# A layer of dilated window attention plus a bilinear GLU on one core: the first 20 microseconds reordered

## The chip, the core and the metric

The kernel runs on one core of a Trainium2 chip. The core has a matrix engine (TensorE, PE in the profile; its weight loads are shown apart as PEld), a vector engine (VectorE, DVE), an engine for activations and copies (ScalarE, ACT), a general one (GpSimd, POOL) and one that only issues transfers (SyncE, SP). ScalarE and GpSimd issue transfers too. All transfers run on 16 DMA engines; those issued from SP go through one queue. An engine works through its instructions in order and waits on semaphores for the others.

The metric is the time of one execution in microseconds of the device; lower is better. The kernel before took 264.84 us, the median of 3 runs (264.83 to 265.99).

## What is computed

Two branches read the same normalized input and are added to it. S = 2048 tokens, D = 640, F = 1536, 32 heads of 20; each token attends to itself and to 7 tokens before it, two apart.

```python
def reference(A_x, A_wqkv, A_wo, B_x, B_w_gate, B_w_up, B_w_down):
    def _A_ref(x, wqkv, wo):
        B, S, D = x.shape
        H = 32; Dh = D // H
        W, dil = 8, 2
        qkv = (lambda x, *d: x.transpose(*d))((x @ wqkv).reshape(B, S, 3, H, Dh), 2, 0, 3, 1, 4)
        q, k, v = qkv[0], qkv[1], qkv[2]
        ...
        logits = jnp.einsum("bhsd,bhswd->bhsw", q, kg) * scale
        logits = jnp.where(mask[None, None, :, :], logits, -1e9)
        attn = _softmax(logits, axis=-1)
        o = jnp.einsum("bhsw,bhswd->bhsd", attn, vg)
        return (lambda x, *d: x.transpose(*d))(o, 0, 2, 1, 3).reshape(B, S, D) @ wo

    def _B_ref(x, w_gate, w_up, w_down):
        g = jnp.einsum("bsd,df->bsf", x, w_gate)
        u = jnp.einsum("bsd,df->bsf", x, w_up)
        h = g * u
        return jnp.einsum("bsf,fd->bsd", h, w_down)

    x = A_x
    xn = _layernorm(x, axis=-1)
    return x + _A_ref(xn, A_wqkv, A_wo) + _B_ref(xn, B_w_gate, B_w_up, B_w_down)
```

Inputs, weights and the result are bfloat16. The inputs fit the core's memory piece by piece; nothing is shared with other cores.

## The kernel before

The tokens are cut into 16 tiles of 128 (x0 to x15) and 4 chunks of 512. Each step of the work is an object with an engine, a cost and the steps that it depends on. A planner (`Plan.order`) computes a due time for every step, backwards from the end, then simulates the engines and always takes, for the engine that is free first, the ready step that is due first. The costs and some earliest ends (`floor`) are written by hand. The order that it finds is the order of the program; no loop is left at run time. "after" puts one step behind another in the plan without a wait between them on the chip.

- A tile of x is loaded (L166), its mean and variance come from two `bn_stats` of 320 columns each (L251) and one `bn_aggr` (L257), epsilon is added (L259), GpSimd raises the sum to the power -0.5 (L265), and VectorE subtracts and multiplies (L270).
- The normalized tile is transposed into `xnT`: for the first chunk on TensorE, in two parts of 3 and 2 blocks (L345), which ScalarE copies out of PSUM (L351); for the other chunks by a DMA transpose that SP issues (L339).
- v comes from `xnT` and `wv` in two halves of 320 columns, five matmuls each (L438); ScalarE copies it (L444), and GpSimd stores it to `vD` in DRAM (L459). q and k come out transposed: five blocks each, five matmuls of 512 columns a block (L405), copied by ScalarE (L412).
- Attention of a chunk: eight products of q with shifted k on VectorE (L476), summed over the head's columns by TensorE with a matrix of ones (L490, two groups), copied (L503), transposed by DMA (L511), softmax on VectorE and ScalarE (L522 to L544); the values of eight positions are gathered from `vD` (L554, 1280 KB a tile), multiplied and summed on VectorE (L579 to L594), and transposed by DMA (L601).
- The GLU of a chunk: 12 blocks of gate and up matmuls of 512 columns (L621), copied (L626) and multiplied (L637). The last step of a tile adds the down projection (L662) and the attention's output projection (L665) in one PSUM bank, and VectorE adds x (L672).

Ahead of all this TensorE runs ten matmuls on zeros (L242) while the first tiles are loaded. The early transfers are spread over two queues. SP issues x0, x1, x2, then wq, x4 to x6, wk, x7, the DMA transposes of chunk 1, wg, x9 to x12, wu, the transposes of the first logits, then the gathered values. ScalarE issues the two column halves of wv, x3 and, later, x8, and loads the table for Exp. `hold` writes two elements of a weight tile so that its load waits for that write. PSUM has six banks under the name `ps`, which all matmuls but the logits' use in turn, and two under the name `pl` for the logits.

The lines that say where a wait or a place comes from:

```python
    HQ = inline("DVE", 0.08, hold(wq))
    WQ = load(10.1, wload(wq, A_wqkv[:, 0:D]), [HQ])
    ...
    qk(0, 0, CS)
    vproj(3)
```

Of the kernel before, what the change touches and what calls it, by code (L numbers as in the profile page):

```python
# [31 lines left out]
class Plan:  # L32
# [15 lines left out]
    def order(self):  # L48
# [4 lines left out]
        for s in reversed(self.steps):  # L53
            s.late = min([t.late for t in s.succ], default=0.0) - s.cost
        for s in self.steps:
            if s.urgent:
                s.late = -1e6 + s.idx
# [40 lines left out]
def kernel(  # L98
# [31 lines left out]
    NS = D // 2  # L130
    BF, F32 = dt.bfloat16, dt.float32
# [16 lines left out]
    mhalf = const.tile([P, 1], F32, name="mhalf")  # L148
    Ek = const.tile([P, KT, H], BF, name="Ek")
# [18 lines left out]

    X = {}
# [4 lines left out]
    def table():  # L174
        dm = sb.tile([P, 1], F32, name="dm", tag="dm")
        nc.vector.memset(dm[:], 0.0)
        nc.scalar.activation(dm[:], dm[:], ACT.Exp)
# [9 lines left out]
    def part(n):  # L187
        src = A_wqkv[:, 2 * D + n * NS : 2 * D + (n + 1) * NS].rearrange("(i p) f -> p i f", p=P)
        return lambda: nc.scalar.dma_start(out=wv[:, :, n * NS : (n + 1) * NS], in_=src)

    def hold(dst):
        return lambda: nc.vector.memset(dst[0:1, 0, 0:2], 0.0)

    X[0] = load(3.0, load_x(0))
    X[1] = load(3.8, load_x(1))
    X[2] = load(4.9, load_x(2))

    def consts0():
        wz = new("wz", [P, CS], BF, "gs", 5)
        nc.vector.memset(wz[:], 0.0)  # L200
        hold(wv)()
        nc.vector.memset(mhalf[:], -0.5)
        make_identity(nc, ident[:])
# [29 lines left out]
    WV = [add("ACT", 4.6, part(0), [C0], occ=0.45)]  # L233
    WV.append(add("ACT", 5.6, part(1), occ=0.45, after=[WV[0]]))
    X[3] = add("ACT", 5.0, load_x(3, nc.scalar), occ=0.45, after=[WV[1]])
    TB = add("ACT", 1.6, table, after=[X[3]])
    CZ = add("POOL", 3.0, consts_z, [C0], occ=1.2)

    def warm():
        ps = psum.tile([P, 512], F32, name="ps", tag="ps", bufs=6)  # L240
        for _ in range(10):
            nc.tensor.matmul(ps[:], lhsT=T["wz"][:, 0:P], rhs=T["wz"][:], start=True, stop=True)  # L242

    main = add("PE", 4.4, warm, [C0])


# [7 lines left out]
    def ln_aggr(t):  # L254
        def fn():
            mv = new(("mv", t), [P, nc.vector.BN_AGGR_DIM], F32, "mv", 6)
            nc.vector.bn_aggr(mv[:], T["st", t][:])  # L257
            ve = new(("ve", t), [P, 1], F32, "ve", 6)
            nc.vector.tensor_scalar(ve[:], mv[:, 1:2], scalar1=EPS, scalar2=None, op0=ALU.add)  # L259
        return fn  # L260
# [17 lines left out]
    def behind(s, a):  # L278
        s.after.append(a)
        s.deps.append(a)  # L280
        plan.steps.remove(s)
        plan.steps.append(s)
# [7 lines left out]

    def aggr_in(t, d):
        GL[t] = inline("DVE", 0.39, ln_aggr(t), [d], 0.35)
        RS[t] = add("POOL", 0.56, ln_rstd(t), [GL[t]])
# [4 lines left out]
    def ln(t):  # L298
        turn = [XT.get(t - (1 if t == CH else 2)), GL.get(t - 1)] if t < 2 * CH else []
        a = add("DVE", 0.48, ln_stats(t, 0), [X[t], GL.get(t - 3), *turn], occ=0.395)  # L300
        a = add("DVE", 0.48, ln_stats(t, 1), [a], occ=0.395)
        a = GL[t] = add("DVE", 0.39, ln_aggr(t), [a], occ=0.3)
        b = RS[t] = add("POOL", 0.56, ln_rstd(t), [a])
        XT[t] = add("DVE", 0.443, ln_apply(t), [b], occ=0.35)
# [13 lines left out]
    XDMA = 4  # L318
    GP = {}

    def transposes(t):
# [19 lines left out]
        def half(g0, g1, n):  # L341
            def pe():
                ps = new(("pst", t, n), [P, KT, P], BF, "ps", 6, psum)
                for g in range(g0, g1):
                    nc.tensor.transpose(ps[:, g, :], T["x", t][:, g * P : (g + 1) * P], ident[:])  # L345

            def ev():
                if n == 0:
                    slot()
                o, i = T["xnT", c][:, g0:g1, q * P : (q + 1) * P], T["pst", t, n][:, g0:g1, :]  # L350
                nc.scalar.copy(o, i)  # L351
            return pe, ev

        if t < CH:
            pa, ea = half(0, 3, 0)
            pb, eb = half(3, KT, 1)
            a = pe_main(0.17, pa, [XT.get((t, 0), XT[t])])
            TX[t] = add("ACT", 0.5, ea, [a], occ=0.42)
            ring.append(TX[t])
            a = pe_main(0.11, pb, [XT[t]])  # L360
            TT[t] = add("ACT", 0.42, eb, [a, TX[t]], occ=0.33)
            if t:
                behind(VE[t - 1][0], TT[t])
            ring.append(TT[t])
        elif t < XDMA:
            a = pe_main(0.28, pe, [XT[t]])
            TT[t] = add("ACT", 0.695, ev, [a], occ=0.6)
            ring.append(TT[t])
        else:
            if c == 1:  # L370
                a = TT[t] = chain[0] = add("SP", 3.0, dma, [XT[t]], occ=1.28, after=[chain[0]])
            else:
                a = TT[t] = add("SP", 2.8, dma, [XT[t], GP.get(c - 2)], occ=1.28, kb=200)
        if t + 5 < W:
            X[t + 5] = load((11.0, 11.5, 14.2)[t], load_x(t + 5), [a])
        elif t == 3:
            X[t + 5] = add("ACT", 6.0, load_x(t + 5, nc.scalar), [a], occ=0.45)
# [18 lines left out]
    def qk(c, lo, n, rs=(0, 1)):  # L396
        for r in rs:
            for j in range(KT):
# [20 lines left out]
                else:  # L419
                    pe_main(3 * one, lambda pe=pe: pe(0, 3), mine)  # L420
                    a = pe_main(2 * one, lambda pe=pe: pe(3, KT), [TT[t] for t in ts], banks=0)
# [6 lines left out]
    VE = {}  # L428

    def vproj(t, ns=(0, 1)):  # L430
        c, q = divmod(t, CH)
        evs = VE.setdefault(t, [])
        for n in ns:
# [15 lines left out]
            if t < 3 and n == 0:  # L449
                pe_main(3 * 0.136, lambda pe=pe: pe(0, 3), [TX[t], WV[n]])  # L450
                a = pe_main(2 * 0.136, lambda pe=pe: pe(3, KT), [TT[t]], banks=0)
            else:
                a = pe_main(KT * 0.136, lambda pe=pe: pe(0, KT), [TT[t], TX.get(t), WV[n]])
            e = add("ACT", 0.425, ev, [a, VS.get(t - 3), CZ], occ=0.35)
            ring.append(e)
# [12 lines left out]
    def prodlog(c):  # L468
# [13 lines left out]
        LASTPW[c] = PW[m]  # L482
        for g in range(2):
# [32 lines left out]
    def softmax(c, hf):  # L516
# [16 lines left out]
        e = add("ACT", 0.635, ex, [DD[n]], occ=0.54)  # L533
# [14 lines left out]
    def load_v8(t):  # L548
# [13 lines left out]
        if t < 3:  # L562
            SPLAST[0] = V8[t]
            V8[t].floor = (43.5, 0, 0)[t]
# [141 lines left out]
    a = st_in(0, 0)  # L706
    a = st_in(0, 1, a)
    aggr_in(0, a)
    a = st_in(1, 0)
    a = st_in(1, 1, a)  # L710
    HQ = inline("DVE", 0.08, hold(wq))
    WQ = load(10.1, wload(wq, A_wqkv[:, 0:D]), [HQ])
    X[4] = load(10.6, load_x(4))
    XT[0, 0] = inline("DVE", 0.31, ln_apply(0, 0, 3 * P), [RS[0]], 0.25)
    XT[0, 1] = inline("DVE", 0.26, ln_apply(0, 3 * P, D), [RS[0]], 0.2)
    XT[0] = XT[0, 1]
# [3 lines left out]
    vproj(0, (0,))  # L720
    a = st_in(2, 0)
    a = st_in(2, 1, a)
    apply_in(1)
    transposes(1)
    WK = load(13.6, wload(wk, A_wqkv[:, D : 2 * D]))
    aggr_in(2, a)
    vproj(0, (1,))
    vproj(1, (0,))
    a = st_in(3, 0)
    a = st_in(3, 1, a)  # L730
    apply_in(2)
    transposes(2)
    aggr_in(3, a)
    behind(VS[0], RS[3])
    vproj(1, (1,))
    vproj(2, (0,))
    apply_in(3)
    transposes(3)
    vproj(2, (1,))
    CE = add("POOL", 1.2, consts_e, [C0, RS[3]])  # L740
    CM = add("POOL", 1.1, consts_m, [CE])
    for t in range(CH, 2 * CH):
# [3 lines left out]
    for t in range(9, 13):  # L746
        X[t] = load(30.0, load_x(t), [TT[t - 5]])
    WL["u"] = load(36.0, wload(wu, B_w_up))
    qk(0, 0, CS)
# [9 lines left out]
    def attention(c):  # L759
# [3 lines left out]
        if c == 0:  # L763
            load_v8(0)
# [54 lines left out]
```

## Time and profile before

| | |
|---|---|
| median of 3 runs | 264.84 us (264.83 to 265.99) |
| profiled execution | 264.88 us |
| its span, first to last instruction | 263.2 us |
| first warm-up to the start of the q matmuls (L405) | 1.27 to 11.73 us |
| end of the last matmul, end of the span | 260.4, 263.2 us |
| x0, x1, x2 land | 3.15, 3.9, 5.7 us |
| halves of wv, wq, wk land | 5.2 and 7.0, 10.3, 13.9 us |
| DVE's products of chunk 0 (L476) | 23.3 to 34.7 us |

The span is what the profiler shows; some 1.7 us lie around it. Busy time is the time in which an engine executes; on TensorE matmuls overlap, so that a matmul's own duration is longer than the distance to the next one. What counts for its pace is that distance. A landing is the time when the semaphore of a transfer has all its counts. The chain of waits goes back from the last instruction and shows at each step what released it.

### The profile page before, as it was taken

What the parts mean: (1) busy time and instruction counts of PE and PEld (TensorE: products, weight loads), DVE (VectorE), ACT (ScalarE), POOL (GpSimd) and SP (SyncE); (2) the same over time, 40 slices, a digit from 0 to 9 for tenths busy, and PEclk for the clock granted to TensorE, in tenths of its full rate; (3) what the DMA queues carried; (4) which work ended last, traced back from release to release, by engine and by line L of the source; (5) the groups of instructions that cost most, each with busy time, mean ns of one, the idle gap of its engine ahead of it and who ended that gap; (6) DMA issues with size and microseconds to landing.
All of it is one profiled execution on the core that took longest, in us unless ns stands there. A gap on an engine that the chain in (4) does not pass through costs nothing.

```text
span 263.2 us, 4101 instructions
## 1 busy us (share of the span) xinstructions
PE 258.5 (98%) x1574; PEld 140.9 (54%) x1574; DVE 214.7 (82%) x337; ACT 106.0 (40%) x197; POOL 39.3 (15%) x84
## 2 busy tenths in 40 slices
PE   7999999999999999999999999999999999999995
PEld 2645455444677446444477554644456764445763
DVE  5775997799899999999999189999992999993221
ACT  2755557555200347455510155655541105554000
POOL 4651036000021121400001000420000004000000
PEclk9999999999999999999999999999999999999999
DMA  7998927999989149931167299451903985111001
GB/s 220 334 198 270 399 106 190 381 362 253 287 188 278 50 99 369 310 112 29 25 124 251 66 305 322 99 149 25 199 28 70 364 296 134 28 25 25 27 25 50
DMA packets 50707, 46.55 MB, mean 177 GB/s; under 512 B 24786, under 2 KB 47840, under 8 KB 50688
## 3 DMA queue, kind: packets, MB, share of 16 engines
q1 hardware_dynamic: 46704, 37.10, 50.1%
q0 software_dynamic: 2384, 8.05, 8.9%
q10 hardware_dynamic: 1600, 1.15, 1.4%
q8 instruction: 12, 0.20, 0.3%
q14 instruction: 7, 0.06, 0.1%
HBM read 35.39 MB, written 5.26 MB: 154 GB/s over the span
## 4 chain that ended last, share of the span: by engine, by line
PE 78%; DVE 11%; DMA 7%; SPq 1%; issue 0%; ACT 0%; DVEq 0%
PE ps L621 30%; PE ps L662 15%; PE ps L405 15%; DMA pv<-vD 7%; PE ps L438 7%; PE ps L665 6%; DVE pv L476 4%; DVE pv L579 3%; PE pl L490 3%; PE ps L242 2%; DVE xr L672 1%; DVE pv L588 1%; SPq L230 1%; DVE pv L592 1%; PE ps L345 0%
## 5 line engine op out<-in xcount | busy, mean ns | idle before, releaser
L621 PE MATMUL ps<-xnT,wg 128*128 128x512 bf16 x240 | 59.6, 379 | 0.0
L621 PE MATMUL ps<-xnT,wu 128*128 128x512 bf16 x240 | 59.6, 379 | 0.0
L662 PE MATMUL ps<-wd,hT 128*128 128x320 bf16 (+2 forms) x384 | 57.4, 299 | 0.0
L476 DVE TENSOR_TENSOR pv<-q,k 128x2560 bf16<-128x2560 bf16 x32 | 46.5, 1484 | 3.0 <-ACT k L412 3.0
L579 DVE TENSOR_TENSOR pv<-pv,a 128x5120 bf16<-128x5120 bf16 x16 | 45.1, 2820 | 3.0 <-DMA pv<-vD 2.9
L662 PEld LDWEIGHTS <-hT 128*128 128x128 bf16 x384 | 37.0, 98 | 16.5 <-issue 0.8
L626 ACT CAST gs<-ps 128x512 bf16<-128x512 f32 x48 | 28.2, 587 | 32.2 <-PE ps L621 32.2
L621 PEld LDWEIGHTS <-wu 128*128 128x128 bf16 x240 | 23.5, 98 | 28.3
L621 PEld LDWEIGHTS <-wg 128*128 128x128 bf16 x240 | 23.5, 98 | 27.7
L626 ACT CAST us<-ps 128x512 bf16<-128x512 f32 x48 | 28.2, 587 | 22.4 <-PE ps L621 22.0
L672 DVE TENSOR_TENSOR xr<-ps,xr 128x320 bf16<-128x320 f32 (+2 forms) x32 | 15.0, 486 | 24.5 <-PE ps L665 16.1
L665 PE MATMUL ps<-wo,oT 128*128 128x320 bf16 (+2 forms) x160 | 27.0, 299 | 0.0
L696 POOL DMA_DIRECT2D out_dram<-xr x14 | 7.6, 542 | 125.8 <-DVE xr L672 119.2
L588 DVE TENSOR_TENSOR pv<-pv 128x2560 bf16<-128x2560 bf16 x16 | 23.8, 1485 | 0.1
L438 PE MATMUL ps<-wv,xnT 128*128 128x320 bf16 x160 | 23.3, 300 | 0.4 <-ACT xnT L351 0.4
L412 ACT CAST q<-ps 128x512 bf16<-128x512 f32 x20 | 11.7, 585 | 27.8 <-PE ps L405 27.8
L637 DVE TENSOR_TENSOR hT<-gs,us 128x512 bf16<-128x512 bf16 x48 | 19.5, 419 | 4.0 <-ACT us L626 4.0
L405 PE MATMUL ps<-xnT,wq 128*128 128x512 bf16 x100 | 22.4, 379 | 0.0
L405 PE MATMUL ps<-xnT,wk 128*128 128x512 bf16 x100 | 22.2, 379 | 0.0
L438 PEld LDWEIGHTS <-xnT 128*128 128x128 bf16 x160 | 15.3, 98 | 7.5 <-ACT xnT L351 0.6
L665 PEld LDWEIGHTS <-oT 128*128 128x128 bf16 x160 | 15.5, 98 | 6.3
L444 ACT CAST v_t<-ps 128x320 bf16<-128x320 f32 x32 | 13.3, 429 | 7.4 <-PE ps L438 4.1
(54 smaller groups left out, 178.7 us busy)
## 6 DMA issues: line engine op xcount, KB each, us to landing
pv<-vD SPq DMA_DIRECT2D x16, 1280.0 KB, 10.0
vD<-v_t POOLq DMA_DIRECT2D x16, 160.0 KB, 4.5
xr<-in_A_x_dram POOLq DMA_DIRECT2D x16, 160.0 KB, 3.7
out_dram<-xr POOLq DMA_DIRECT2D x14, 160.0 KB, 3.5
wg<-in_B_w_gate_dram SPq DMA_DIRECT2D x1, 1920.0 KB, 8.1
wu<-in_B_w_up_dram SPq DMA_DIRECT2D x1, 1920.0 KB, 12.2
wd<-in_B_w_down_dram SPq DMA_DIRECT2D x1, 1920.0 KB, 17.7
x<-in_A_x_dram SPq DMA_DIRECT2D x11, 160.0 KB, 4.9
```

The source lines that it names most:

```text
L405: nc.tensor.matmul(T[key][:, 0:n], lhsT=(wk if r else wq)[:, i, j * P : (j + 1) * P], rhs=T["xnT", c][:, i, lo : lo + n], start=(i == 0), ...
L438: nc.tensor.matmul(T["psv", t, n][:, 0:NS], lhsT=T["xnT", c][:, i, q * P : (q + 1) * P], rhs=wv[:, i, n * NS : (n + 1) * NS], start=(i == ...
L444: nc.scalar.copy(T["v_t", t][:].rearrange("p (j h) -> p j h", j=Dh, h=H)[:, :, n * H // 2 : (n + 1) * H // 2], T["psv", t, n][:, 0:NS].rea ...
L476: nc.vector.tensor_tensor(T["pw", c, i // 2][:, i % 2, :, :], T["q", c][:], T["k", c][:, :, DIL * i : DIL * i + CS], ALU.mult)
L579: nc.vector.tensor_tensor(v[:].rearrange("p w (j h) -> p w j h", j=Dh, h=H), v[:].rearrange("p w (j h) -> p w j h", j=Dh, h=H), T["a", n][ ...
L588: nc.vector.tensor_tensor(v[:, 0:4, :], v[:, 0:4, :], v[:, 4:8, :], ALU.add)
L621: nc.tensor.matmul(ps[:], lhsT=(wu if r else wg)[:, i, f * P : (f + 1) * P], rhs=T["xnT", c][:, i, :], start=(i == 0), stop=(i == KT - 1))
L626: nc.scalar.copy(s[:], T[key][:])
L637: nc.vector.tensor_tensor(h[:], T["gs", c, f][:], T["us", c, f][:], ALU.mult)
L662: nc.tensor.matmul(ps, lhsT=T["hT", c, f][:, q * P : (q + 1) * P], rhs=wd[:, f, sl], start=(f == 0), stop=(f == FT - 1 and not wo_part))
L665: nc.tensor.matmul(ps, lhsT=T["oT", t][:, g, :], rhs=wo[:, g, sl], start=False, stop=(g == KT - 1 and f1 == FT))
L672: nc.vector.tensor_tensor(T["xr", t][:, sl], T["psD", t, n][:, 0:w], T["xr", t][:, sl], ALU.add)
```

## The change

1. x0 is loaded as two column halves of 320, each with its own transfer; each `bn_stats` waits for its half.
2. The halves of wv become row blocks 0 to 2 and 3 to 4, and they, x3 and x8 are issued by SP instead of ScalarE. SP's order is now x0 (two), x1, x2, wv (two), wq, x3 to x6, wk, x7, the transposes, wg, x8 to x12, wu. `hold` is gone. The value matmuls of x0 to x2 go through the row blocks in parts: blocks 0 and 1 of both column halves, block 2 of both, then blocks 3 and 4.
3. For x0 to x2, epsilon, power and add are replaced by a Sqrt with a bias on ScalarE and a reciprocal on VectorE. ScalarE loads the table for Sqrt first and the one for Exp after the first q columns.
4. The parts of the transposes on TensorE are 2 and 3 blocks, in the `pl` banks. x3 is transposed by DMA like later tiles.
5. q and k of chunk 0 are computed for 384 columns (x0 to x2) and then for 128 (x3).
6. The gathered values of tile 0 are issued right behind wu, ahead of the transposes of the logits.
7. Eight warm-ups, and a ninth behind the transposes of x0.
8. The planner walks the steps in the order of their dependences instead of the order of their making.

```diff
-        for s in reversed(self.steps):
+        todo = {s: len(s.succ) for s in self.steps}
+        work = [s for s in self.steps if not s.succ]
+        while work:
+            s = work.pop()
             s.late = min([t.late for t in s.succ], default=0.0) - s.cost
+            for d in s.deps:
+                todo[d] -= 1
+                if not todo[d]:
+                    work.append(d)
...
+    TA, VA = 2, 3
...
+    def load_x0(g):
+        def fn():
+            if g == 0:
+                new(("x", 0), [P, D], BF, "x", 5)
+            nc.sync.dma_start(out=T["x", 0][:, g * NS : (g + 1) * NS], in_=x_flat[0:P, g * NS : (g + 1) * NS])
+        return fn
...
     def part(n):
-        src = A_wqkv[:, 2 * D + n * NS : 2 * D + (n + 1) * NS].rearrange("(i p) f -> p i f", p=P)
-        return lambda: nc.scalar.dma_start(out=wv[:, :, n * NS : (n + 1) * NS], in_=src)
-
-    def hold(dst):
-        return lambda: nc.vector.memset(dst[0:1, 0, 0:2], 0.0)
-
-    X[0] = load(3.0, load_x(0))
+        i0, i1 = ((0, VA), (VA, KT))[n]
+        src = A_wqkv[i0 * P : i1 * P, 2 * D : 3 * D].rearrange("(i p) f -> p i f", p=P)
+        return lambda: nc.sync.dma_start(out=wv[:, i0:i1, :], in_=src)
+
+    X0 = load(2.75, load_x0(0))
+    X[0] = load(3.2, load_x0(1))
     X[1] = load(3.8, load_x(1))
-    X[2] = load(4.9, load_x(2))
+    X[2] = load(4.4, load_x(2))
+    WV = [load(5.5, part(0)), load(6.6, part(1))]
+    WQ = load(9.7, wload(wq, A_wqkv[:, 0:D]))
+    X[3] = load(10.1, load_x(3))
+    X[4] = load(10.5, load_x(4))
...
-        for _ in range(10):
-            nc.tensor.matmul(ps[:], lhsT=T["wz"][:, 0:P], rhs=T["wz"][:], start=True, stop=True)
+        new("wps", [P, 512], F32, "ps", 6, psum)
+        warming(8)
...
+    def ln_std(t):
+        def fn():
+            nc.scalar.activation(new(("std", t), [P, 1], F32, "ve", 6)[:], T["mv", t][:, 1:2], ACT.Sqrt, bias=epst[:])
+        return fn
+
+    def ln_inv(t):
+        return lambda: nc.vector.reciprocal(new(("rstd", t), [P, 1], F32, "rstd", 6)[:], T["std", t][:])
...
-    XDMA = 4
+    TPE = CH - 1
...
-        if t < CH:
-            pa, ea = half(0, 3, 0)
-            pb, eb = half(3, KT, 1)
...
+        if t < TPE:
+            pa, ea = half(0, TA, 0)
+            pb, eb = half(TA, KT, 1)
...
+        if c == 0:
+            load_v8(0)
         for g in range(2):
...
-    a = st_in(0, 0)
-    a = st_in(0, 1, a)
+    a = st_in(0, 0, X0)
+    a = st_in(0, 1)
     aggr_in(0, a)
+    inv_in(0)
+    XT[0, 0] = inline("DVE", 0.26, ln_apply(0, 0, TA * P), [RS[0]], 0.2)
+    XT[0] = XT[0, 1] = inline("DVE", 0.31, ln_apply(0, TA * P, D), [RS[0]], 0.25)
     a = st_in(1, 0)
     a = st_in(1, 1, a)
-    HQ = inline("DVE", 0.08, hold(wq))
-    WQ = load(10.1, wload(wq, A_wqkv[:, 0:D]), [HQ])
-    X[4] = load(10.6, load_x(4))
...
     transposes(0)
-    vproj(0, (0,))
+    pe_main(0.22, lambda: warming(1), banks=0)
+    vproj(0, (-1, 0))
...
-    for t in range(9, 13):
+    for t in range(8, 13):
         X[t] = load(30.0, load_x(t), [TT[t - 5]])
     WL["u"] = load(36.0, wload(wu, B_w_up))
-    qk(0, 0, CS)
+    qk(0, 0, TPE * P)
+    qk(0, TPE * P, P)
+    TE = add("ACT", 1.6, table(ACT.Exp), [Q[0][1]], occ=1.5)
     vproj(3)
```

## The prediction

> **What bounds the kernel now.** I read the page's busy times first:
>
> ```profile
> PE 258.5 (98%) x1574; PEld 140.9 (54%) x1574; DVE 214.7 (82%) x337; ACT 106.0 (40%) x197; POOL 39.3 (15%) x84
> ```
>
> TensorE (PE) is busy 258.5 of 263.2 us. The chain of waits, in order of time, shows from when on it never stops (start us, length us, what):
>
> ```profile
> 1.27 4.45 PE ps L242 x10
> 5.72 0.44 PE ps L345 x3
> 6.16 0.02 issue
> 6.19 0.49 ACT xnT L351
> 6.67 0.05 issue
> 6.72 0.94 PE ps L438 x5
> 7.66 0.28 PE ps L345 x5
> ...
> 11.89 10.79 PE ps L405 x50
> 22.68 1.36 PE ps L438 x10
> ```
>
> Ten warm-ups, the transposes of x0, a wait for ScalarE's copy, then matmuls back to back. The first five value matmuls take 0.77 us from 6.72 to the transposes at 7.49; later ones take 0.136 each (1.36 for ten). Warm-ups of 512 columns start 0.427 apart, q matmuls of 512 columns 0.216. So PE ran at half speed until about 6.95, though the clock column of the windows view reads 1.00 throughout.
>
> The list of waits (us in total, times, longest) has one more PE wait, at a logit group, and the timeline of PE (start, length, operation, idle before) prices it against the same group of the first chunk:
>
> ```profile
> PE pl L490 <- DVE pv L476: 0.3, 1, 0.3
> ```
>
> ```profile
> 36.12 2.34 PE L490 MATMUL pl<-pv,Ek 128*32 128x512 bf16 x40
> 38.39 0.85 PE L438 MATMUL ps<-wv,xnT 128*128 128x320 bf16 x5
> ```
>
> ```profile
> 91.26 1.48 PE L490 MATMUL pl<-pv,Ek 128*32 128x512 bf16 x23
> 93.05 1.24 PE L490 MATMUL pl<-pv,Ek 128*32 128x512 bf16 x17 [0.32 <-DVE pv L476]
> 94.22 1.25 PE L405 MATMUL ps<-xnT,wq 128*128 128x512 bf16 x5
> ```
>
> To the next group's start it takes 38.39 - 36.12 = 2.27 undisturbed and 94.22 - 91.26 = 2.96 here: the last products of VectorE (DVE) cost PE 0.69 us. DVE was late because it had waited twice for values:
>
> ```profile
> 42.10 0.29 DVE L522 TENSOR_TENSOR m<-LT 128x256 bf16<-128x256 bf16 x1 [0.62 <-DMA LT<-L]
> 49.03 2.83 DVE L579 TENSOR_TENSOR pv<-pv,a 128x5120 bf16<-128x5120 bf16 x1 [1.33 <-DMA pv<-vD]
> 72.86 2.83 DVE L579 TENSOR_TENSOR pv<-pv,a 128x5120 bf16<-128x5120 bf16 x1 [1.61 <-DMA pv<-vD]
> ```
>
> So time can come only from before 11.73, where the q matmuls start, from PE's work itself, and from the 0.69.
>
> **x0 and its normalization.** x0 (160 KB) is issued at 0.82 and lands 2.3 later, at 3.15; x1, as large and issued 0.45 later, lands at 3.90. 160 KB of stream thus cost 0.75, half of it 0.38: the first half lands near 2.8 (bounds 2.6, by a whole 0.75 less one issue, and 3.15, no gain), the second near 3.2. Two statistics take 0.89 together and now end near 3.7 instead of 4.06. Before, the add (0.15), the power on POOL (0.56) and the handovers took 0.90 from the aggregate's end (4.31) to the normalization (5.21). Now Sqrt on ScalarE and a reciprocal on DVE: the only 128x1 activation took 0.20, the power 0.56; for the reciprocal 0.15 (the 128x1 add) and 0.55 (the reciprocal of 128x64) are the bounds. I take 0.20 and 0.17, plus two handovers of 0.1: 0.57. The 256-column normalization (0.34) then ends near 4.86, and the transposes start near 4.9 instead of 5.65.
>
> The Trainium skill, page "DMA: Bandwidth & Descriptors" (section Anatomy of one DMA), says that a DMA costs a fixed 2.0 us plus its bytes at 436 GB/s, nearly all of it waiting for the receipt; the whole x0 fits that (2.38 against 2.3), but a half would land only 0.2 earlier, at 3.0. By it the chain gains some 0.2 less, and the sum below 0.1 less.
>
> **Eight warm-ups, a ninth later.** Eight end at 1.27 + 8 x 0.427 = 4.69. PE idles to 4.9; two transposes, three more behind the second normalization (near 5.55), the ninth to 5.97. The copies of x0 (0.38 and 0.48) lie beside it; the first is done near 5.8. Value matmuls start near 6.0 instead of 6.72. At half speed 0.95 us hold 3.6 of them; eight (before x1's transposes now, five before) are done at 6.92 + 4.4 x 0.136 = 7.52, against 7.49. DVE's x1 is ready near 7.25, so it is covered by 0.27. The gain of the early start is eaten by the half clock: three matmuls.
>
> **Loads in one queue.** Values' weights move from ScalarE's queue (issued 1.27) to SyncE's (SP), behind four x loads of 0.45 each: issued near 2.6. Ahead of the first part's end lie x0 to x2 (480 KB) and itself (480 KB). At the 370 GB/s of 4 to 5 us after x2 (near 4.5) it lands at 5.8, at x1's pace (160 KB in 0.75) at 6.7. I take 5.9, since the queue is never empty then; it is covered to 6.0, and each 0.1 later costs about 0.05. The second part (0.9 behind) and wq (2.2 more: 9.0; 10.3 at worst) are covered to 7.4 and 11.3; wk, issued after x1's transposes, to 15.4 (before: issued 8.35, landed 13.9).
>
> **From x1's transposes to q.** Before: 11.73 - 7.49 = 4.24. x3's five transposes leave PE (-0.28); three value matmuls are already done (-0.41). ScalarE's copies now hold Sqrt x2 (0.20) between them, and only two value matmuls stand between x1's transposes and its first copy: a wait of 0.19 and one of 0.05. 4.24 - 0.28 - 0.41 + 0.24 = 3.79, from 7.52: q starts at 11.31, **0.42 earlier** (bounds 0, and 0.7 with PE at full clock from 6.0, when x1 at 7.25 limits).
>
> **q and k as 384 + 128.** Matmuls cost 0.0558 at 128, 0.1358 at 320, 0.2158 at 512 columns: a line, 0.1625 at 384. 50 x (0.1625 + 0.0558 - 0.2158) = **+0.13**. The table load for Exp (1.28) and its 0.2 sit behind two q copies; PE makes a q bank in 0.81, the copy takes 0.48, six banks: no wait. Were the cover gone, 1.5. x3's transposed copy must be there when 128 columns start, at 11.31 + 8.1 = 19.4. x3 is normalized near 13; the first DMA transpose took 5.0 to land, so near 18.
>
> **Values 0 behind wu.** In SP's order that load now waits for nothing but its stores and follows wu, landed at 35.2, while DMA moved 158 GB/s from 33 to 36 and 8 from 36 to 38. At the 5.5 us between the first two value loads' landings (48.94, 54.49) it is there near 41. Behind it stand the logits' transposes (needed at 42.1). It leaves the busy stretch from 41 to 73, so both DVE waits (2.94) go. Against that DVE gets x8's normalization behind the products, since x8 is now loaded behind wg: 0.89 + 0.21 + 0.15 + 0.43, less overlap, 1.6, of which the idle 0.62 and 0.73 before 42.1 absorb 1.35. DVE is some 2.7 ahead at 93, PE 0.3: **-0.69** (bounds 0, if DVE stays as late, and 0.69).
>
> **Waits and edits taken at nothing.** Sqrt waits on ScalarE for DVE's aggregate; behind it stand the copies of x0 (Sqrt x0, not yet needed) and the second copy of x1 (Sqrt x2: the 0.20 above). The reciprocal waits on DVE for Sqrt; behind it stand only the same tile's normalization and x1's statistics, whose load lands near 4.0. Before, x1's statistics ran in that wait, which is why x1 gains little. The two 1x1 memsets (0.06 each) go and one of epst comes, beside the warm-ups; the transposes now use the two logit banks, free until 36. On SP, x3's transpose (1.26) and x8's load (0.5) move wg's and wu's issues some 1 us later; wg landed at 28.3 and wu at 35.2 for a use after 42. POOL loses the powers of x0 to x2; a store of values (0.6) now stands before x3's power and one behind it, so x3 is normalized near 13, as said. The planner's new loop gives due times, and the order it makes after q and k of chunk 0 is the old one but for five value matmuls.
>
> **Sum.** -0.42 + 0.13 - 0.69 = -0.98. The profiled execution took 264.88 (span 263.2, 1.7 around it; the median is 264.84): **263.9 us**. The rest of PE's order is unchanged.
>
> **Rivals.**
> 1. Half clock for longer, the slower side. Place: the first value matmul at 6.0. For: the load of their weights may land at 6.7 to 6.9, and two warm-ups are gone, so PE would idle for almost 1 us before the clock has risen. Against: at 6.95 it rose although PE was busy only 0.64 us of 6 to 7. If the wait of 5.7 us from the first warm-up to full speed begins again in part, to between 9.7 and 12.5, PE does half the work from 6.9 on: 1.4 against 3.0 by 9.7 (+1.6), 2.8 against 5.8 by 12.5 (+3.0). With the rest as forecast, 265.5 to 266.9, middle 266.2. It decides if the weights land after about 6.5. The Trainium skill's page "TensorE: Matmul & The Clock Gate" (The HAM clock gate) names such a rule: full speed comes after a busy window of 3.4 us, free-running, so one window missed costs 3.4 us at half speed; 6.95 + 3.4 gives 10.35, and 265.8. 15%.
> 2. Nothing gained in the middle, or x3's or x4 to x7's transposed copies late: five transposes of 1.26 on SP instead of four; the last landed at 22.4 for a need at 23.9, and moves to about 23 for a need at 23.7. Either costs about 0.7: 264.6. For: POOL's order puts two stores (0.6 each) around x3's power. 20%.
> 3. PE at full clock from the start of the values, x0's halves at their lower bounds, neither copy wait: 0.26 + 0.2 + 0.24 more, 263.2. For: nothing ties the clock's rise to the program. Against: it takes all three. 13%.
>
> **Chances.** The forecast 52%, its own range 263.4 to 264.5. The range 263.2 to 266.1 reaches into rivals 3 and 1. What a measurement can tell from no change is about 0.5%, 1.32 us, or below 263.52 and above 266.16. Faster: 0.52 x 0.15 + 0.13 x 0.8 + a little of rival 2 = 0.20. Slower: half of rival 1, and 5% for delays that the trace doesn't show: 0.13. Same: 0.67.
>
> **What would show it.** q's first matmul near 11.3 (step 1 wrong if after 11.8); value matmuls 0.136 apart from 7 on (else rival 1); the logit group of chunk 1 in 2.27; no DVE wait for values at 48 and 72; q and k of chunk 0 in 10.9 without a gap at 19.4 or 23.7. The forecast falls if PE stops anywhere after 12 us, or if the weights of the values are what it waits for at 6.

## The result, and the profile after

The changed kernel took **267.24 us** (median of 20 runs, 265.15 to 268.86) against 265.01 (20 runs, 264.43 to 266.86): a ratio of 1.0072, interval [1.0057, 1.0087]. It is slower by 0.7%, clear of the interval, and the time lies above the range of the prediction.

The profiled execution is its best, 265.15 (span 263.4). The page's busy times:

```profile
PE 257.5 (98%) x1618; PEld 142.9 (54%) x1618; DVE 214.9 (82%) x336; ACT 108.8 (41%) x210; POOL 37.8 (14%) x81
```

PE is busy for 1.0 us less than before. The chain of waits over the first 13 us (start, length, what) shows where the start went (it lets a matmul begin at the end of the one before it, so the q matmuls stand at 12.34 here; the timeline, by which the text goes, has 12.18):

```profile
2.19 0.43 SPq L175
2.62 0.04 issue
2.66 4.48 DMA wv<-in_A_wqkv_dram
7.14 0.04 issue
7.18 1.35 PE ps L462 x8
8.53 0.28 PE pl L377 x5
...
10.44 1.90 PE ps L462 x14
12.34 0.81 PE ps L429 x5
```

Before, the chain ran through warm-ups, transposes and ScalarE's copy. Now it runs through SyncE's fourth load and then through one transfer, the first part of wv: issued at 2.66, landed at 7.14. The q matmuls start at 12.18, against 11.73 before and 11.31 in the prediction. The list of PE's waits (us, times, longest) names the same thing:

```profile
PE ps L462 <- DMA wv<-in_A_wqkv_dram: 0.9, 1, 0.9
```

The middle of the kernel came out as forecast. PE's timeline at the logit group of chunk 1, then DVE's at the two products that had waited for values:

```profile
91.84 2.34 PE L525 MATMUL pl<-pv,Ek 128*32 128x512 bf16 x40
94.11 1.25 PE L429 MATMUL ps<-xnT,wq 128*128 128x512 bf16 x5
```

```profile
49.36 2.82 DVE L614 TENSOR_TENSOR pv<-pv,a 128x5120 bf16<-128x5120 bf16 x1
...
71.15 2.82 DVE L614 TENSOR_TENSOR pv<-pv,a 128x5120 bf16<-128x5120 bf16 x1
```

The group takes 94.11 - 91.84 = 2.27 in one piece (2.96 before), and neither product carries an idle time (1.33 and 1.61 before).

I split the span of every trace into three pieces: up to the first q matmul (the start), from there to the start of the last matmul (the middle), and the rest (the end). Before: 11.73 + 248.46 + 2.99. After: 12.18 + 247.90 + 3.37. So the middle gained 0.56, the start lost 0.45 and the end 0.38: 0.27 more, 265.15 for 264.88. That is the best execution; the median lies 2.1 above it. The tables of the windows view (window, span, then the busy share of PE, PEld, DVE, ACT and POOL, granted clock, DMA share, GB/s) show what the queue did; before, then after:

```profile
3.00:4.00 1.00, 1.00 (x4) 0.41 (x3) 0.82 (x2) 1.00 (x1) 0.00 (x0) 1.00 0.95 271
4.00:5.00 1.00, 1.00 (x4) 0.30 (x2) 0.93 (x5) 0.39 (x2) 0.41 (x1) 1.00 1.11 370
5.00:6.00 1.00, 1.00 (x6) 0.34 (x5) 0.96 (x6) 0.00 (x0) 0.15 (x1) 1.00 1.08 348
```

```profile
3.00:4.00 1.00, 1.00 (x4) 0.39 (x3) 0.52 (x2) 0.00 (x0) 0.86 (x3) 1.00 0.88 293
4.00:5.00 1.00, 0.85 (x2) 0.00 (x0) 0.58 (x3) 0.29 (x1) 0.02 (x1) 1.00 0.73 145
5.00:6.00 1.00, 0.58 (x6) 0.34 (x6) 0.99 (x4) 0.27 (x1) 0.00 (x0) 1.00 1.04 384
```

From 4 to 5 us, between x2's stream and wv's, DMA moved 145 GB/s, where two queues had moved 370. The stream ran nearly dry just where the prediction says that the queue is never empty.

### The profile page after: what moved, and what is told of

It is laid out like the page before. It is cut to its first block, busy times and chain, and to the rows that moved or that the text cites. A ratio compares the mean times of both kernels' runs of the same rounds, so it can differ in the third digit from the quotient of the medians.

```text
span 263.4 us, 4203 instructions
## 1 busy us (share of the span) xinstructions
PE 257.5 (98%) x1618; PEld 142.9 (54%) x1618; DVE 214.9 (82%) x336; ACT 108.8 (41%) x210; POOL 37.8 (14%) x81
## 4 chain that ended last, share of the span: by engine, by line
PE 96%; DMA 2%; SPq 1%; issue 0%; DVE 0%
PE ps L656 39%; PE ps L697 20%; PE ps L429 16%; PE ps L462 8%; PE ps L700 8%; PE pl L525 3%; DMA wv<-in_A_wqkv_dram 2%; SPq L175 0%; SPq L182 0%; PE pl L377 0%; DVE xr L707 0%
## 5 line engine op out<-in xcount | busy, mean ns | idle before, releaser
L436 ACT CAST q<-ps 128x512 bf16<-128x512 f32 (+2 forms) x25 | 12.2, 501 | 26.0 <-PE ps L429 26.0
L429 PE MATMUL ps<-xnT,wq 128*128 128x512 bf16 (+2 forms) x125 | 22.6, 336 | 0.0
L429 PE MATMUL ps<-xnT,wk 128*128 128x512 bf16 (+2 forms) x125 | 22.5, 336 | 0.0
L429 PEld LDWEIGHTS <-wk 128*128 128x128 bf16 x125 | 11.2, 98 | 10.5
```

Source lines behind the costliest of these rows:

```text
L429: nc.tensor.matmul(T[key][:, 0:n], lhsT=(wk if r else wq)[:, i, j * P : (j + 1) * P], rhs=T["xnT", c][:, i, lo : lo + n], start=(i == 0), ...
L436: nc.scalar.copy(dst, T[key][:, 0:n])
```

## The experiments

Theory A: the weights of the values land late, because they stand behind four loads of x in one queue. B: eight warm-ups leave PE idle before and after x0's transposes, and the clock rises late, whatever the weights do. C: another part of the change costs it. E came later: the program's end costs more. All runs follow. A time is the median of 5 to 12 executions (20 for the first two rows), and a ratio is to the kernel before as it was timed beside that run, where its median was 264.76 to 264.88. Then come the readings of each profiled execution: "clock" is when the trace's record of the granted clock begins, at full speed (nothing is recorded ahead of it, which is why the windows view shows 1.00 from the first microsecond on); "wv" is the landing of its first part, left out where its loads are as before; then the three pieces of the span.

| run | time, median (range) | ratio to before | profiled | clock | wv | q starts | middle | end |
|---|---|---|---|---|---|---|---|---|
| before | 265.01 | | 264.88 | 6.92 | 5.23 | 11.73 | 248.46 | 2.99 |
| after | 267.24 (265.15 to 268.86) | 1.0072 | 265.15 | 4.81 | 7.14 | 12.18 | 247.90 | 3.37 |
| e1_wv_act | 266.3 (265.02 to 266.44) | 1.0041 [1.0027, 1.0055] | 266.37 | 10.63 | 5.28 | 13.40 | 247.90 | 3.36 |
| e2_warm5 | 265.56 (264.72 to 267.07) | 1.0029 [1.0013, 1.0044] | 265.18 | 4.66 | 7.26 | 12.22 | 247.90 | 3.36 |
| e3_before_v8 | 264.34 (264.08 to 264.81) | 0.9982 [0.9973, 0.9991] | 264.81 | 4.50 | | 12.34 | 247.77 | 2.99 |
| e4_before_8warm | 265.43 (264.19 to 266.27) | 1.0013 [0.9996, 1.0029] | 265.99 | 9.73 | | 13.14 | 248.12 | 3.00 |
| e5_warm10_3 | 265.93 (264.97 to 266.24) | 1.0038 [1.0025, 1.005] | 266.24 | 5.47 | 7.57 | 13.27 | 247.90 | 3.37 |
| e6_wv_first | 266.74 (266.42 to 268.68) | 1.009 [1.0067, 1.0113] | 266.57 | 6.33 | 6.10 | 12.73 | 248.76 | 3.37 |
| e7_after_again | 264.86, one run | | 264.86 | 4.95 | 6.84 | 11.86 | 247.90 | 3.38 |
| e8_v8_sqrt | 264.64 (264.58 to 264.67) | 0.9997 [0.9989, 1.0006] | 264.66 | 7.14 | | 12.17 | 247.78 | 2.99 |
| e9_after_third | 265.1 (264.72 to 266.81, and one of 268.81) | 1.001 [0.9994, 1.0026] | 264.72 | 6.52 | 6.71 | 11.72 | 247.90 | 3.36 |
| e10_wv_behind_table | 266.53 (266.32 to 266.93) | 1.0061 [1.0048, 1.0075] | 266.32 | 5.80 | 5.44 | 12.49 | 248.76 | 3.37 |
| e11_before_onequeue | 265.1 (264.58 to 265.86) | 1.0008 [0.9997, 1.002] | 265.35 | 5.96 | 7.04 | 12.56 | 248.11 | 2.97 |
| f1_after_a | 267.0 (265.04 to 268.61) | 1.0073 [1.0043, 1.0102] | 268.40 | 13.83 | 7.91 | 15.43 | 247.90 | 3.36 |
| f2_warm10_3_again | 265.41 (264.9 to 266.42) | 1.0025 [1.0011, 1.0038] | 265.79 | 4.57 | 7.79 | 12.81 | 247.90 | 3.38 |
| f3_after_b | 266.05, one run | | 266.05 | 10.22 | 6.67 | 13.04 | 247.90 | 3.38 |
| f4_after_c | 266.45, one run | | 266.45 | 10.39 | 7.29 | 13.44 | 247.90 | 3.38 |
| g1_after_wd7 | 265.34, one run | | 265.34 | 5.60 | 7.71 | 12.73 | 247.90 | 3.02 |
| g2_v8_wd3 | 264.49 (264.43 to 264.94) | 0.9989 [0.998, 0.9998] | 264.94 | 5.73 | | 12.09 | 247.77 | 3.36 |
| g3_v8_again | 264.2 (264.06 to 264.45) | 0.9975 [0.9966, 0.9985] | 264.22 | 6.87 | | 11.74 | 247.78 | 3.00 |

### One part undone or done alone

**e1: wv issued by ScalarE again.** wq is held back with `hold` again, x3 and x4 follow it, and the table for Sqrt is loaded behind wv.

```diff
-    WV = [load(5.5, part(0)), load(6.6, part(1))]
+    WV = [add("ACT", 4.6, part(0), [C0], occ=0.45)]
+    WV.append(add("ACT", 5.6, part(1), occ=0.45, after=[WV[0]]))
...
+    HQ = inline("DVE", 0.08, hold(wq))
+    WQ = load(9.7, wload(wq, A_wqkv[:, 0:D]), [HQ])
```

> The changed kernel with the value weights issued by ScalarE at 1.27 again and wq held back until x0 is normalized, as before; all else as changed. Theory A (the weights of the values land late behind four x loads in one queue; TensorE stands still for 1.1 us at 6.1, and in most executions its clock falls or rises late in that gap): the first part lands by 5.8, values start near 6.1, q near 11.4; median 264.0 to 264.6 us, spread no larger than that of the kernel before (2.4 us). Theory B (eight warm-ups are too few, whatever the weights do): median stays above 266. Theory C (another part of the change, such as the table load, the split or the DMA transpose of x3, costs the time): median 266 to 267, with a gap after 12 us in the trace.

The weights land at 5.28 and PE never waits for them. But they share the engines with x: x0's second half lands at 4.24, x1 at 5.77 (4.09 in the changed kernel), so that PE now waits 1.12 for x0 instead. PE's timeline (start, length, operation, idle before):

```profile
5.97 0.79 PE L379 MATMUL pl<-ident,x 128*128 128x128 bf16 x5 [1.12 <-DVE x L295]
6.55 0.63 PE L265 MATMUL ps<-gs 128*128 128x512 bf16 x1
6.98 2.34 PE L464 MATMUL ps<-wv,xnT 128*128 128x320 bf16 x8
```

Eight value matmuls take 2.34 where they took 1.35: half speed, until 10.63. The wait for the weights is gone and the median stays at 266.3, above 266 as B had it; A alone doesn't carry the loss.

**e2: five warm-ups instead of one behind x0's transposes.**

```diff
-    pe_main(0.22, lambda: warming(1), banks=0)
+    pe_main(0.22, lambda: warming(5), banks=0)
```

> The changed kernel with five warm-ups instead of one behind the transposes of x0, which fill TensorE's gap until the value weights land. Theory A in both its parts: values still start near 7.2, so no execution gets faster than the best of the changed kernel (265.15), but the clock has no gap to fall in: median 265.2 to 265.6, spread under 1.5 us. If the late landing alone cost the time and the clock nothing: median stays 267.2. Theory B: in between, since the gap from 4.6 to 5.4 stays: 266 to 267. Theory C: 267.

The median is 1.7 below the changed kernel's 267.24, but that shows little by itself, since the unaltered kernel gave 265.1 another time (e9, below). The trace still has wv at 7.26 and q at 12.22: the weights stay late. What the idle time costs is read from f1 and f2 below, which were timed side by side.

**e3: values 0 behind wu, alone, in the kernel before.**

```diff
+        if c == 0:
+            load_v8(0)
         for g in range(2):
```

> The kernel before, with the gathered values of tile 0 issued right behind wu and nothing else changed. If the logit group of chunk 1 waits for VectorE because of the late values: the wait of 0.69 us goes, median 264.3 (ratio 0.9974). If moving that load only delays the transposes of the logits: same or up to 0.5 slower.

Faster by 0.18%, and the fastest version here; the middle is 0.69 shorter (248.46 to 247.77), as the prediction had it. A late start alone shortens the middle too, to 248.12 and 248.11 in e4 and e11, and e3's q starts late. But the same kernel in g3, where q starts at 11.74 as before, has 247.78.

**e4: eight warm-ups, alone, in the kernel before.**

```diff
-        for _ in range(10):
+        for _ in range(8):
```

> The kernel before with eight warm-ups instead of ten. x0 is ready at 5.65 in either, so TensorE stands still from 4.66 to 5.65. Theory B: the clock rises later or falls back in that gap, median 266 or more, with a spread of 3 us. Theory A: the weights are there at 5.2, the gap is covered; median within 0.4 us of the kernel before.

Its times fall into two groups of this one kernel: five of 12 between 264.19 and 264.77, the other seven from 265.09 to 266.27; the kernel before, timed beside it, has 265.35 as the highest of 32. In the profiled one, 265.99, PE is idle from 4.7 to 5.73, ahead of x0's transposes, and the clock is full only from 9.73. So B holds with the old loads too; by the times, in some executions and not in others.

**e11: wv (in column halves) and x3 in SyncE's queue, alone, in the kernel before.**

```diff
     X[2] = load(4.9, load_x(2))
+    WV = [load(5.9, part(0)), load(6.8, part(1))]
+    X[3] = load(7.3, load_x(3))
```

> The kernel before with one part of the change: the value weights (still in column halves) and x3 issued by SyncE behind x2, everything else as before, ten warm-ups included. Theory A: the first half, 400 KB, issued near 2.2, lands 4.3 later, near 6.5, or later, after a stretch of less than 200 GB/s; value matmuls start at 6.7 to 7.1 and, since the second half is wanted right after x1's transposes, q starts at 11.8 to 12.3; time 264.9 to 265.4. As the prediction had it (the stream never empty): landing at 5.6, no change, 264.76. Theory B alone: no change either, since the ten warm-ups are kept.

The first half, 400 KB, is issued at 2.20 and lands at 7.04; before, issued at 1.27 in the other queue, at 5.23. DMA moves 200 GB/s from 3 to 4 and 172 from 4 to 5. PE waits 0.85 and q starts 0.83 later in this trace, which is A without any other part of the change. The median moves by 0.2 only, within the interval.

**e8: values 0 behind wu and Sqrt for x0, in the kernel before.**

```diff
+        if t == 0:
+            s = add("ACT", 0.3, ln_std(t), [GL[t], TB], occ=0.3)
+            RS[t] = inline("DVE", 0.17, ln_inv(t), [s], 0.16)
+            return
...
+    TE = add("ACT", 1.6, table(ACT.Exp), [Q[0][1]], occ=1.5)
```

> The kernel before with two parts of the change: the gathered values of tile 0 issued right behind wu, and x0 alone (not x1 and x2) normalized by way of Sqrt on ScalarE and a reciprocal, with the table for Exp loaded after the second q copy. From the sum: values behind wu gave 264.34 alone. Sqrt takes 0.295 and the reciprocal 0.164 in the changed kernel, with handovers 0.6 against 0.9, so x0 is normalized 0.3 earlier; TensorE takes it up at the end of the tenth warm-up, 5.5, and q starts 0.1 to 0.2 earlier: 264.2 to 264.3. Rival: x1's statistics, which ran beside the power on GpSimd, now start 0.4 later, x1 is normalized later and q starts 0.2 later: 264.5 to 264.6.

0.3 above e3: the rival of that expectation. x1's statistics no longer run beside the power: they start at 5.41 (4.50 in g3), x1 is normalized from 7.43 (6.95), and PE waits 0.22 for it.

### Both gaps closed, and the queue's order

**e5: ten warm-ups ahead, three behind.**

```diff
-        warming(8)
+        warming(10)
...
-    pe_main(0.22, lambda: warming(1), banks=0)
+    pe_main(0.22, lambda: warming(3), banks=0)
```

> The changed kernel with ten warm-ups ahead of x0's transposes instead of eight and three behind them instead of one; loads and the rest as they are. Theory A+B (the time above the best phase is the clock's, lost because TensorE stands idle around 5 and around 6.5; the weights of the values still land near 7.1): transposes at 5.5, warm-ups to about 7, no idle stretch over 0.3 before the value matmuls start near 7.2; the q matmuls start near 12.2 in nearly every execution, the times lie close together (within about 0.8) and their median is 265.2, about 0.3 over the kernel before. Theory A alone with the clock blameless (the weights' lateness is all of it, whatever TensorE does in the gap): 267 as before, with the same spread. Theory B alone (late weights cost nothing once the warm-ups are there): 264.2, q at 11.5. Theory C (another part of the change costs 2): 267, with the loss somewhere behind 12.2.

No run shows the loss of 2 us, and all but one (264.97) lie some 1 us or more above the old time beside it, 264.76. PE's timeline of the profiled execution, at full clock from 5.47:

```profile
7.61 0.97 PE L462 MATMUL ps<-wv,xnT 128*128 128x320 bf16 x6 [0.96 <-DMA wv<-in_A_wqkv_dram]
9.20 0.43 PE L462 MATMUL ps<-wv,xnT 128*128 128x320 bf16 x2 [0.61 <-DMA wv<-in_A_wqkv_dram]
```

Both parts of wv are waited for, and q starts at 13.27 without a matmul at half speed behind 5.5. This is A by itself: 266.24.

**e6: wv's first part ahead of x1, its second ahead of x2** (on top of e5).

```diff
+    WV = [load(4.9, part(0))]
+    X[1] = load(5.3, load_x(1))
+    WV.append(load(6.0, part(1)))
+    X[2] = load(6.5, load_x(2))
```

> The run before this one (ten and three warm-ups) with the order in SyncE's queue changed: x0 in two halves, the first part of the value weights, x1, their second part, x2. Theory A (the first part is late because four transfers of x stand ahead of it in one queue): it lands near 6.0 instead of 7.1, x1 near 5.5 to 6.3, value matmuls start near 6.5 to 7.0, q starts between 11.7 and 12.0; time 264.5 to 264.9. If instead x1, now behind 480 KB, becomes the last arrival (normalized after 8.2), TensorE waits for x1's transposes and q stays at 12.2 or later: 265.2 to 265.8. If the queue is slow whatever its order (its first transfers all land late), the weights land after 6.6 all the same and nothing is gained: 265.2.

The weights land at 6.10, as A says, but the bare second moves forward with them: DMA moves 95 GB/s from 3 to 4, x0's second half lands at 4.16 and x1 at 6.55. The list of PE's waits:

```profile
PE pl L378 <- DVE x L294: 0.8, 2, 0.6
PE ps L698 <- DVE hT L673: 0.7, 1, 0.7
```

The first is the wait for x0 and x1. The second is not about loads: the planner, given other costs, orders the products of gate and up otherwise, and the middle is 0.86 longer. Its time is to be read without that: 265.9.

**e10: wv issued by ScalarE behind its table load** (on top of e1, ten and three warm-ups).

```diff
+    TB = add("ACT", 1.6, table(ACT.Sqrt))
+    WV = [add("ACT", 4.0, part(0), after=[TB], occ=0.45)]
+    WV.append(add("ACT", 5.0, part(1), occ=0.45, after=[WV[0]]))
```

> The changed kernel with ten and three warm-ups, and the two parts of the value weights issued by ScalarE again, but behind its table load, near 2.3 instead of 1.27, so that x0's halves are out of the way; wq waits until x0 is normalized. Theory A in its sharper form (in one queue a large transfer brings a bare stretch of 1 us at half the rate before its own stream starts; in a second queue that stretch lies beside the stream of x1 and x2): x0's halves land by 3.3, the first part of the weights by 6.4, q starts at 11.6 to 12.0, time 264.4 to 264.9. If the start of a large transfer holds up every queue, x1 and x2 land 0.5 to 1 later than in the changed kernel, the weights after 6.8, and the time is 265.3 to 266.

It didn't test what it was to test: the transfers left at 1.27 all the same, while the table load ran from 0.80 to 2.08; here it didn't hold them. As in e1 the weights are early (5.44), and x0, x1 and x2 late (3.90, 5.87, 7.14). It has e6's 0.86 in the middle too.

### The changed kernel again

**e7, e9, f1, f3, f4** are the changed kernel unaltered, **f2** is e5 again, beside f1. Expected, in this order:

> The changed kernel once more, unaltered, for a second profile of another execution: the time is a draw from its 20 runs (265.2 to 268.9). Theory A+B: if this execution takes more than 266, its value matmuls run at half speed (0.267 apart instead of 0.136) in a stretch between 6 and 13 and q starts after 13; if it takes 265.2 to 265.5, the clock is up before 7 and stays. Theory C: a time over 266 with q at 12.2 and a gap later on.

> The changed kernel unaltered, timed beside the two next runs on one chip. Theory A+B (late weights, and a clock that some executions raise late or lower again in the gaps): times from 264.9 to above 267, median 266 to 267.3; in the profiled execution the weights' first part lands between 6.8 and 7.6 and DMA moves less than 200 GB/s between 4 and 5. If the 267.24 belonged to the executions measured first and not to the kernel, the median is 264.8 to 265.4, as the single execution of 264.86 suggests.

> The changed kernel unaltered, on one chip beside its version with ten and three warm-ups. So far it took 267.24 (20 runs), 264.86 (one run) and 265.10 (11 runs, three of them from 266.0 to 268.8). Theory A+B: two groups of times, one from 264.7 to 265.5 and one above 266, and the runs above 266.7 are those with a mean clock below 0.995 or, in a trace, with value matmuls 0.267 apart. If the late weights are all of it, the times form one group and go with the landing of the weights (6.7 to 7.6), no more than 1.2 apart.

> The changed kernel with ten and three warm-ups, again, now beside the unaltered one. Theory A+B: no run above 266.6 and no mean clock below 0.998; the lowest times are those of the unaltered kernel plus 0.2 to 0.5 (the third warm-up ends at 7.2 or later), so that it is better only where the unaltered one has many runs above 266.7. If the clock isn't what makes the slow runs, this one has as many of them.

> The changed kernel unaltered, one more execution with its trace. Theory A+B: above 266.5 its trace shows value matmuls 0.267 apart between 7 and 12; below 265.5 it shows none behind 7.2. If the late weights are all of it, a time above 266.5 comes with matmuls 0.136 apart and the weights landing after 8.5.

(f4 as f3.) Timed twice on one chip, the unaltered kernel gave 265.1 and 267.0: times from 264.7 to 268.6 in two mixtures. Three traces show what sets them apart. PE's timeline in e9 (264.72), f3 (266.05) and f1 (268.40):

```profile
5.51 0.63 PE L263 MATMUL ps<-gs 128*128 128x512 bf16 x1
6.75 1.33 PE L462 MATMUL ps<-wv,xnT 128*128 128x320 bf16 x8 [0.60 <-DMA wv<-in_A_wqkv_dram]
7.92 0.44 PE L377 MATMUL pl<-ident,x 128*128 128x128 bf16 x5
```

```profile
5.54 0.63 PE L263 MATMUL ps<-gs 128*128 128x512 bf16 x1
6.72 2.29 PE L462 MATMUL ps<-wv,xnT 128*128 128x320 bf16 x8 [0.54 <-DMA wv<-in_A_wqkv_dram]
8.80 0.74 PE L377 MATMUL pl<-ident,x 128*128 128x128 bf16 x5
```

```profile
5.64 0.63 PE L263 MATMUL ps<-gs 128*128 128x512 bf16 x1
7.96 2.29 PE L462 MATMUL ps<-wv,xnT 128*128 128x320 bf16 x8 [1.69 <-DMA wv<-in_A_wqkv_dram]
10.04 0.74 PE L377 MATMUL pl<-ident,x 128*128 128x128 bf16 x5
...
13.24 2.36 PE L462 MATMUL ps<-wv,xnT 128*128 128x320 bf16 x14
```

e9 and f3 do the same things at the same times up to 6.75: the same landing, the same gap. In e9 the clock rose at 6.52, in f3 at 10.22, and q starts 1.32 apart. f1 has the late landing as well, and the clock at 13.83, when the values are nearly through: 3.71 later than e9. f2, timed beside f1 on the same chip, has no run above 266.42 where f1 has six of nine: the warm-ups take off 1.6 of its median, 0.6 over the kernel before remain. So the loss is A and B together: the landing opens the gap, and the clock, depending on the execution, can make it more than twice as dear (q starts 1.31 later than before in f3 for a wait of 0.54, and 3.70 later in f1 for 1.69). C falls for this loss, since the middle is 247.90 in each of these traces; what is left of it is 0.37, and lies at the end.

### The end of the program

In each trace with the change the end is 0.37 longer. After the last store SyncE waits for the semaphores of all transfers, in nine steps of a fixed order, some 0.06 each where nothing is left to wait for. The changed kernel has two transfers more on these semaphores, x0's second half and x3's transpose. They are dealt out in turn, so the last store's semaphore moved from the second to last of these steps to the second. Seven steps stand behind it instead of one, and 6 x 0.06 is the 0.37. **g1** is the changed kernel with wd in seven transfers, which moves the semaphore on to the second to last step again; **g2** is e3 with wd in three, `at` being (0, 4, 8, FT), which moves it to the second; **g3** is e3 again. The edit of g1:

```diff
+    def wd_load():
+        at = (0, 2, 4, 6, 8, 10, 11, FT)
+        for a, b in zip(at, at[1:]):
+            src = B_w_down[a * P : b * P, :].rearrange("(i p) f -> p i f", p=P)
+            nc.sync.dma_start(out=wd[:, a:b, :], in_=src)
```

> The changed kernel with wd loaded by seven transfers instead of one, so that the last store's semaphore moves on by six places: from the one that SyncE waits for second at the end of the program (eight more waits follow it, some 0.06 each) to one that it waits for second to last. Theory E (the closing waits cost the changed kernel 0.36 that the prediction left out): from the start of the last matmul to the end of the span 2.95 to 3.05 instead of 3.32 to 3.39. If it is something else at the end, it stays above 3.3. The time itself is a draw and says nothing here.

> The kernel before with values 0 behind wu, and wd loaded by three transfers, so that the last store gets the semaphore that SyncE waits for second: nothing else of the changed kernel. Theory E: last matmul to the end 3.32 to 3.39 instead of 2.98, and the median 0.3 to 0.4 above that of the run with one transfer for wd. If the two more transfers cost or save something elsewhere, the last matmul starts at another time than 260.1 while q starts the same.

> The kernel before with values 0 behind wu alone, once more beside the run before it: 264.1 to 264.4, ratio to the kernel before 0.998, last matmul to the end 2.98.

The end is 3.02 in g1 and 3.36 in g2, and g2's median is 0.29 above g3's. SyncE's wait for the last store (us, times, longest), in the changed kernel and in g1:

```profile
SPq L844 <- DMA out_dram<-xr: 1.1, 1, 1.1
```

```profile
SPq L850 <- DMA out_dram<-xr: 0.7, 2, 0.5
```

In the first, one wait of 1.1, with seven steps still behind it; in the second most of the list is worked off while the stores land. E holds in both directions.

## Why the prediction was wrong

- **x0 and its normalization**: right where its second half is on time. The first half landed at 2.62 to 2.84 (forecast 2.8). The fit on the Trainium skill's page "DMA: Bandwidth & Descriptors" (Anatomy of one DMA) gives 3.0, which is too late here; the page states that fit for transfers that GpSimd issues, and x0 is issued by SyncE. The second half came at 3.15 to 3.33 in seven of the ten traces with this queue order (forecast 3.2), at 3.64 to 3.92 in three. Sqrt took 0.29, not 0.20, the reciprocal 0.16, and the handovers only 0.11 in all, not 0.20: that the sum came out (0.56 for 0.57) is in part luck. Transposes started at 4.88 to 5.06 with the half on time (4.9), at 5.41 to 5.64 without.
- **Loads in one queue: the step that failed**: "I take 5.9, since the queue is never empty then". In ten traces the first part landed at 6.67 to 7.91, all but one past the bound of 6.7. First, the queue does run almost empty: wv's transfer, issued at 2.66, reached full rate only at 5.0, some 2.3 us later (the one issued at 1.71 in e6 at 4.0), and x2's stream had ended near 4.2. The row to go by was in the trace of before: 400 KB from issue at 1.27 to landing at 5.23, 3.96. Put behind the new issue, 2.66, that gives 6.6, and 6.8 with 80 KB more, where the rate of a stream in full flow gave 5.9. Second, a transfer has landed only with the last of its 16 counts, and that one came late. In the ten traces the eighth count came at 6.24 to 6.41 and the last 0.3 to 1.5 us behind it; in f1 fifteen were there by 6.70, the last at 7.91, and one packet of that trace, begun at 5.23, took 1.18 us where most take 0.055. The prediction had no term for such a straggler, and what holds it up is not shown.
- **Eight warm-ups, a ninth later**: value matmuls at 6.0 became 6.72 to 7.96, by the landing.
- **From x1's transposes to q**: right. 3.79 forecast, 11.72 - 7.92 = 3.80 in e9, 12.18 - 8.37 = 3.81 in the profile after; but it set out from 7.92 and 8.37 there, and later in most other traces, not from 7.52. Instead of -0.42, the start came to between 0 and +3.7.
- **q and k as 384 + 128, values 0 behind wu**: right. +0.13 - 0.69 = -0.56, and the middle went from 248.46 to 247.90. x3's transposed copy was there at 18.41, needed at 20.3; the table for Exp cost PE nothing.
- **"The rest of PE's order is unchanged"** is true, but the sum took the end of the span over from before: +0.37 was left out.
- **Rival 1 is what happened, in part of the executions.** Its condition, weights after about 6.5, held in every one of the ten traces, so 15% was the mis-sized landing once more. But the condition doesn't decide it: in e7, e9 and the profile after the clock had risen by 6.52 all the same. Its price was right where the clock missed one chance (265.5 to 266.9 forecast; 266.05 and 266.45 in f3 and f4) and too low where it missed two (f1: 268.40, full clock at 13.83, later than the 12.5 allowed for). The Trainium skill's rule, page "TensorE: Matmul & The Clock Gate" (The HAM clock gate), gave 10.35 and 265.8 for one missed window; the trace of f3 has 10.22 and 266.05. It agrees.

Put together for the best execution, e9: start -0.01, middle -0.56, end +0.37 make 264.7, and it took 264.72. For the median, 267.24, the start has to be about 2.6 later than before's 11.73, which is between f4 and f1. One thing stays open: of the first 20 runs, ten had a mean clock of 0.991 to 0.994, lower than f1's 0.999, and took 266.73 to 267.72. Since the record begins with the rise, such a mean says that the clock, once up, was down again; by my estimate for 3 to 5 us (twice 0.006 to 0.009 of some 266). No trace caught one, so when and why it fell is open. None of 110 runs of the kernel before that were timed beside the experiments has a mean under 0.999, and none of the 30 of e2, e5 and f2, which have more warm-ups (one of e6 has: 0.993, at 268.68).

## What to carry to other kernels

Price a transfer that is moved by its row from issue to landing, put behind its new issue, and not by the rate of a stream that is already running. Where PE has a gap near the start, its price can be the clock and not the gap: fill it with warm-ups on both sides before anything else is shortened, and look at several executions, since one profile may show the harmless one. And when transfers are added or taken away, look at which semaphore the last store gets.

## What the runs showed of the hardware

- **When the clock rises.** The full-clock stretches that the 20 traces record last 252.59, 256.00 or 259.41 us, which is 74, 75 or 76 steps of 3.413. In all 20 the clock rose at the end of a stretch of 3.413 us in which PE had stood idle for at most 0.97 (0.70 in the kernel before, 0.97 in e9). Reckoned back from there in steps of 3.413, each stretch that passed without a rise held 0.86 or more (1.17 in f3, 1.43 in f4, 1.46 and then 0.96 in f1). (Idle is counted here as what the columns of the matmuls, at the clock of the time, leave over.) So the stretch needn't be without a gap; about a quarter of it is forgiven, and between 0.86 and 0.97 both were seen. And the steps begin anywhere: 4.50 in e3 and 6.87 in g3 with the same kernel. The Trainium skill's page "TensorE: Matmul & The Clock Gate" (The HAM clock gate) has the same window of 3413 ns, free-running, and puts the cost of the ramp below 1% of a typical kernel's span; here one kernel on one chip took 264.72 and 268.40, 1.4% apart, for the ramp and the landing together.
- **The start of a large transfer.** Between the issue of a weight load and its full stream lies a stretch in which few packets move: 145 GB/s (after, 4 to 5), 95 (e6, 3 to 4), 78 (e1, 7 to 8, ahead of wq), and single packets take up to 0.7 us in the first of these, against 0.055 in the stream. In the changed kernel's own wq, issued at 3.67 behind wv's stream, it doesn't show.
- **The last of 16 counts** sets the landing: 6.67 to 7.91 in the ten traces, where the eighth count had come at 6.24 to 6.41.
- **The order of the closing waits** is worth 0.37 us.
